# P·V with V as the weights on four column strips, O kept transposed, in a one-core adaLN + sliding-window attention + gMLP kernel

## The chip, the cores and the metric

One NeuronCore of a Trainium2 chip runs the whole program. The metric is the device time of one execution in microseconds, 278.81 us in the median of three runs before the change (278.15 to 280.09). Engine names follow the profile: PE is TensorE's matmul stream, PEld its weight loads, DVE is VectorE, ACT ScalarE, POOL GpSimd, SP SyncE (here only a queue that issues DMAs).

## The reference

One block over x of 2048 tokens by 448: a modulation from c, then attention, then a gMLP.

```python
mod = (_silu(c) @ w_mod)                      # six vectors: sa, ca, ga, sb, cb, gb
h = _layernorm(x) * (1 + ca) + sa
x = x + ga * _A_ref(h, A_wqkv, A_wo)
h = _layernorm(x) * (1 + cb) + sb
x = x + gb * _B_ref(h, B_w_in, B_w_sp, B_b_sp, B_w_out)

# _A_ref: 16 heads of width 28, query i sees keys i-255 .. i
scores = einsum('bhqd,bhkd->bhqk', q, k) * 28 ** -0.5
scores = where((i - j >= 0) & (i - j < 256), scores, -1e9)
o = einsum('bhqk,bhkd->bhqd', softmax(scores), v);  return o @ wo
# _B_ref: z = gelu(x @ w_in); z1, z2 = halves; z2 = layernorm(z2)
#         g = w_sp @ z2 + b_sp;  return (z1 * g) @ w_out
```

## The kernel before

Tokens stand in 16 tiles of 128. The attention works tile by tile (`j`, L794) and in two halves of the heads (L800); a half is two groups of four heads, `qi`. Heads are padded from 28 to 32 columns.

**How the order is set.** The program is a list of steps (`add`, L131), numbered as they are created, each with the engines it may run on and a cost. No loop runs in program order: the string `ORDER` (L19) lists every step as `number.engine.slots`, with p, a, v, g, s for PE, ACT, DVE, POOL and SP, and the slots of the buffers it takes. `order` (L148) replays that list, one in-order program for each engine; `count` and `waits` (L190, L209) derive the semaphores from the steps' dependencies. The costs in the code do not act on the chip; ORDER does.

**Head.** x, the modulation weights and WQ/WK are loaded by SP and ACT (L411 to L421: on ACT's queue first w_mod, then c), DVE and POOL clear pads, and PE runs matmuls on an identity (`warm`, L554). Layernorm statistics (`stats`, L589: `bn_stats`, `bn_aggr`, then two POOL steps at L597 and L600) and `norm` (L606) give xn; PE transposes it (L666), ACT or DVE applies the modulation while copying it to `hT` (L678, L680); then Q, K and V for the 512 tokens (L696, L708, L743, L756), evicted by ACT or DVE (L718/L719, L748/L749, L760/L761). V goes to `Vaug` with a column of ones at place 28 of each head's 32 (L493, L494), so that P·V also gives the softmax's sum.

**Attention of a tile with three key blocks** (j >= 2), for each half:

- S transposed (keys on partitions) for two head groups goes to PSUM banks 0 to 3, one bank for each of the four heads, by 36 matmuls of 32 rows (L858): first 4 of 128 keys by 128 queries for the middle block and 16 of 128 keys by 64 queries, then 16 of 64 keys by 64 queries, which use half of the columns of the array. Only the parts of the two outer blocks that the window can reach are computed. The middle block of the second head group is one more matmul (L867, `QBD` holds Q block-diagonally) into bank 5.
- ACT takes the exponential of both (L819, 2048 and 512 columns) to `PW`. Banks 0 to 3 have one place in rotation (`bW`), so S of the next half waits for this exponential.
- DVE masks the triangles: one pass for each head group, from `PW` to `PT` (`mask_all`, L872, L874).
- PE forms P·V (L901) with P as the weights (128x128) and V as the moving operand (32 columns): three matmuls for each head, 24 in a half, into bank 4 (`bO`, one place).

After both halves DVE takes the reciprocal of the 16 sums (L915), scales O while copying it to `o_sb` (L917), a DMA transpose on SP's queue puts it into `hT` (L923, the issue is at L468), and PE multiplies by wo (L926). x is updated (L931), normalised again, transposed by DMA (L937) and scaled (L949, L951).

**gMLP.** z2 (L1011) and z1 transposed (L1032) with gelu on ACT (L1018, L1040), statistics and normalisation of z2 on DVE (L592, L1023), the spatial product (L1055) and the output product (L1072). z2 shares its place with `PW`, so the gelu waits for all P·V.

Of the kernel before, what the change touches and what calls it, by code (L numbers as in the profile page):

```python
# [19 lines left out]
2.a 24.v 33.g 0.s 25.v 26.v 27.v 36.g 37.g 3.a 1.s 34.g 4.a 31.g 28.v 5.s 35.g 8.a 29.v 38.g 6.s 9.a 7.s 43.a 39.g 53.p.1 54.p.2 55.p.3 44.p.0 130.v  # L20
128.v 131.v 129.v 132.g 45.a 46.a 56.p.4 57.p.5 58.p.6 59.p.7 60.p.2 52.p.1 139.v 137.v 140.v 138.v 133.g 134.v 141.v 136.a.0 142.g 135.a.1 143.v
120.v 145.v.2 108.v 107.v 67.p.3 146.p.2 144.a.3 68.p.0 69.p.4 147.p 150.p.3 40.g 123.g 121.g 122.v 148.v 149.v 151.p 152.a 48.a 70.p.0 71.p.0
154.p.4.5.6.7 155.p 156.p 153.a 158.p 125.g 42.g 160.p 159.p 157.p 162.a 164.a 32.g 41.g 124.g 47.v 10.s 11.s 14.s 127.g 126.v 191.v 192.v 187.v 30.v
49.g 50.g 13.s 15.s 16.s 12.s 161.a 169.p.0 170.a 171.p.1 172.a 346.p.0 347.a.0 163.v 185.v 189.v 186.v 188.v 190.v 51.v 175.p.7 173.p.6 112.p.0
114.p.1 193.g 194.g 199.g 201.g 197.g 200.g.0 195.g 176.v 202.v.1 198.v.2 113.v 196.g.3 350.v 174.a 352.p.0 353.a.1 181.p.7 203.p.0 371.p.0 166.s
167.s 165.s 168.s 17.s 348.v 115.v 206.p.1 177.p.6 204.v 205.v 207.v 109.p.0 372.a.2 373.a 182.a 208.a 378.p.0 379.a.3 380.a 239.v 241.v 243.v 237.v
244.v 110.v 238.v 20.s 19.s 18.s 240.v 242.v 354.v 111.v 178.v 179.p.7 183.p.1 211.p.0 184.v 293.v 356.v 180.v 349.p.0 398.p.0 212.a 351.p 355.p
215.p.1 357.p 400.p.0 209.p.0 399.a.4.0 381.v 291.v 216.v 406.p.0 210.a 245.g 246.g 251.g 252.v.0 358.v 359.v.0 376.v 374.v 253.g 249.g 254.g.1 403.v
221.p.1 213.p.0 383.v 214.v 402.v 294.v 375.p.0 377.p 407.a.5.1 401.a 427.p.0 222.a 408.p.0 382.p 223.p.0 225.p.1 428.a.6.2 435.p.0 409.a 411.v
429.p.0 384.p 258.s 118.g 247.g 250.g.2 256.s 257.s 248.g.3 255.s 262.g 259.g 226.a 436.a.0.3 292.v 224.v 295.v 385.v 386.v.1 229.p.0 227.p.1 404.p.0  # L30
410.v 297.v 228.v 430.a 456.p.0 230.a 457.a.1.4 360.s 218.s 219.s 220.s 217.s 432.v 261.v 260.v 437.p.0 233.p.0 231.p.1 405.p 412.p 296.v 232.v 438.a
234.a 464.p.0 413.p 275.p.1 263.p.0 458.p.0 465.a.2.0 431.v 298.v 116.g 299.g 119.g 300.g 117.g 307.g 305.g 306.g.0 301.g 308.g.1 302.g.2 439.v 414.v
415.v.2 264.v 469.v 440.v 460.v 468.v 276.a 459.a 485.p.0 486.a.3.1 433.p.0 265.p.1 434.p 441.p 466.p.0 493.p.0 266.a 467.a 303.g 304.g.3 442.p
235.p.0 489.v 443.v 444.v.0 494.a.4.2 461.v 487.p.0 269.p.1 514.p.0 236.a 488.a 462.p.0 277.p.0 463.p 470.p 471.p 495.p.0 515.a.5.3 522.p.0 270.v
490.v 497.v 416.s 387.s 472.v 473.v.2 278.a 267.p.1 268.v 498.v 491.p.0 492.p 361.p.0 362.v 523.a.6.4 526.v 363.v 496.a 543.p.0 544.a.0.0 516.p.0
388.p.1 499.p 279.p.0 389.v 548.v 547.v 517.a 280.a 551.p.0 552.a.1.1 500.p 417.p.1 524.p.0 281.p.0 501.v 518.v 418.v 502.v.1 527.v 519.v 525.a 282.a
572.p.0 573.a.2.2 283.p.1 545.p.0 520.p.0 521.p 528.p 529.p 310.s 309.s 445.s 311.s 474.s 312.s 271.s 274.s 273.s 272.s 503.s 580.p.0 284.a 546.a
581.a.3.3 419.v 556.v 555.v 530.v 531.v.0 576.v 364.v 475.p.0 289.p.1 553.p.0 549.p.0 550.p 476.v 601.p.0 554.a 290.a 557.p 574.p.0 558.p 287.p.0
285.p.1 602.a.4.4 477.v 577.v 584.v 420.v 559.v 390.v 560.v.2 478.v 286.v 313.v 391.v 421.v 288.a 575.a 609.p.0 610.a.5.0 504.p.0 314.g 315.g 365.g
366.g 316.g 367.g 368.g.0 578.p.0 323.p.1 582.p.0 479.v 505.v 585.v 605.v 506.v 324.v 630.p.0 583.a 631.a.6.1 446.p.0 579.p 586.p 603.p.0 319.p.1  # L40
587.p 604.a 611.p.0 392.g 480.g 481.g 393.g 394.g 422.g 423.g 395.g.1 396.g 424.v.2 369.v 425.v 447.v 588.v 589.v.1 448.v 614.v 449.v 606.v 613.v
320.a 612.a 638.p.0 639.a.0.2 22.s 532.s 23.s 561.s 21.s 426.s 397.s 317.p.0 329.p.1 632.p.0 607.p.0 659.p.0 318.a 330.v 333.p.0 321.p.1 633.a 642.v
660.a.1.3 322.a 325.s 327.s 328.s 326.s 640.p.0 608.p 641.a 334.v 507.v 634.v 667.p.0 668.a.2.4 664.v 615.p 533.p.0 616.p 562.p.1 661.p.0 643.v 635.v
617.v 618.v.0 563.v 671.v 619.s 688.p.0 662.a 636.p.0 637.p 644.p 645.p 669.p.0 331.p.1 689.a.3.0 696.p.0 670.a 332.a 697.a.4.1 564.v 534.v 646.v
535.v 663.v 647.v.2 693.v 565.v 692.v 536.v 701.v 672.v 335.p.0 337.p.1 690.p.0 665.p.0 338.a 691.a 717.p.0 718.a.5.2 339.p.1 698.p.0 666.p 673.p
674.p 590.s 648.s 828.s 482.g.2 450.g 508.g 451.g 452.g 509.g 537.g 538.g 566.g 539.g 453.g.1 454.g 510.g 340.v 700.v 620.p.1 675.v 483.v 676.v.0
370.s 455.s 540.g.0 567.g 568.g 541.g 814.g 699.a 719.p.0 336.a 720.a 725.p.0 694.p.0 695.p 702.p 703.p 591.p.0 727.p.0 726.a.6.3 728.a 746.p.0
747.a.0.4 721.v 722.v 621.v 704.v 705.v.1 729.v 592.v 730.v 593.v 750.v 622.v 677.s 723.p.0 341.p.1 724.p 731.p 748.p.0 342.a 749.a 754.p.0 732.p
343.p.0 756.p.0 678.p.1 755.a.1.0 757.a 733.v 751.v 623.v 734.v.2 775.p.0 484.s 758.v 759.v 752.p.0 753.p 760.p 761.p 706.s 829.s 542.s 735.s 511.g.1
624.g 569.g.2 512.g 679.v 762.v 763.v.0 777.p.0 776.a.2.1 344.a 778.a 649.p.1 780.v 779.v 650.v 783.p.0 707.p.0 781.p.0 782.p 785.p.0 513.s 812.g  # L50
813.g 811.g 570.g 625.g 626.g 627.g.0 594.v 680.v 681.v 651.v 652.v 784.a.3.2 787.v 786.a 788.v 860.p.0 861.p.1 862.p 789.p 790.p 864.a 653.v 682.g
628.g 683.g 684.g 708.v 685.v.1 595.v 791.v 792.v.1 654.g 655.g 686.g 764.s 571.s 345.s 629.s 736.p.1 765.p.0 656.g.2 817.v 793.s 766.v 767.v 737.v
768.v 818.v 709.v 738.v 815.a 863.p 871.a 878.p.2 879.p.0 880.p 881.p 882.a 889.a 596.g 657.g 597.g 816.g 896.p.3 897.p.1 898.p 899.p 900.a 1012.p.2
794.p.0 914.p.0 907.a 658.s 687.s 769.g 598.g.0 599.g 770.g 600.s 739.v 872.v 710.v 865.v 866.v 711.g 712.g 771.g 713.g 772.v.2 773.v 740.v 741.g
774.s 867.v 795.v 809.g 714.g.1 742.g 796.v 715.v 822.v 884.v 797.v 798.v 891.v 902.v 743.g.0 744.g 799.g 716.s 745.s 800.g 801.v.2 890.v 868.v 883.v
# [210 lines left out]
def bass_adaLN_cond__sliding_block__mixer_gmlp__prompt_kernel(  # L266
# [888 lines left out]
```

## Time and profile before

| | us |
|---|---|
| median of 3 runs | 278.81 (278.15 to 280.09) |
| the profiled execution | 279.08, of which its span is 277.4 |
| PE busy | 266.4 (96%) |
| DVE, ACT, POOL busy | 164.4, 128.2, 127.2 |
| S of the first tile starts; last P·V starts | 18.7; 111.5 |
| first spatial matmul (L1055) | 156.6 |

The granted TensorE clock is 1.00 throughout. The span has three stretches: the head to about 25 us, the attention to about 111 us, in which the products of Q, K and V and the out-projection are mixed in, and then the gMLP. A busy time is the union of the engine's records; small matmuls overlap in the array, so their records' durations add up to more than the time that they take. What a matmul takes is read from the distance of its start to the next one's. In a group's line the numbers after the bar are busy us, mean ns of one, and idle time ahead of it.

### The profile page before, as it was taken

How to read it: one execution, taken by the hardware profiler on the slowest of the kernel's cores; microseconds unless marked ns; L12 is line 12 of the kernel's file. 1: busy time of each engine (PE TensorE's matmuls, PEld its weight loads, DVE VectorE, ACT ScalarE, POOL GpSimd, SP SyncE). 2: the span in 40 equal slices, each digit the busy share in tenths (PEclk: the TensorE clock that was granted, in tenths of full speed). 3: DMA queues.
4: the chain of work that ended last, by engine and by line, in shares of the span. 5: the costliest groups of instructions: out<-in, count | busy, mean ns of one | idle time of the engine just before them, and what ended most of it. 6: DMA issues, size and time to landing. Idle time of an engine off the chain costs nothing.

```text
span 277.4 us, 7383 instructions
## 1 busy us (share of the span) xinstructions
PE 266.4 (96%) x3198; PEld 140.8 (51%) x3225; DVE 164.4 (59%) x364; ACT 128.2 (46%) x154; POOL 127.2 (46%) x191
## 2 busy tenths in 40 slices
PE   4999999999999999999999999999999999999995
PEld 1636466656576766444444444444444444444452
DVE  5679999989989999679798300300320042025434
ACT  2587999999999999577676600000000000000000
POOL 6831826914725669884949000600571065334110
PEclk9999999999999999999999999999999999999999
DMA  7966142145993666834999999100000000001113
GB/s 208 304 170 205 23 91 47 21 80 96 121 225 79 80 80 97 194 77 83 190 176 205 206 197 187 35 0 0 0 2 0 0 0 2 0 0 56 62 50 99
DMA packets 65843, 26.01 MB, mean 94 GB/s; under 512 B 56466, under 2 KB 64723, under 8 KB 65811
## 3 DMA queue, kind: packets, MB, share of 16 engines
q1 hardware_dynamic: 65168, 24.68, 43.4%
q10 hardware_dynamic: 642, 0.86, 1.1%
q8 instruction: 25, 0.41, 0.6%
q14 instruction: 8, 0.06, 0.1%
HBM read 9.01 MB, written 1.84 MB: 39 GB/s over the span
## 4 chain that ended last, share of the span: by engine, by line
PE 82%; DVE 8%; DMA 4%; POOL 3%; issue 1%; ACT 0%; ACTq 0%; SPq 0%; POOLq 0%
PE ps L1055 35%; PE ps L1032 8%; PE ps L1072 7%; PE ps L1011 6%; PE ps L708 5%; PE ps L901 5%; PE ps L858 3%; DMA hT<-xn 3%; PE ps L926 3%; PE ps L756 3%; PE ps L867 2%; DVE st_all L592 2%; PE ps L557 1%; DMA c_row<-in_c_dram 1%; PE ps L696 1%; POOL hT L951 1%
## 5 line engine op out<-in xcount | busy, mean ns | idle before, releaser
L819 ACT ACTIVATE PW<-ps 128x2048 bf16<-128x2048 f32 (+1 forms) x56 | 67.4, 1242 | 2.9 <-PE ps L867 1.1
L1059 DVE TENSOR_TENSOR tmpg<-ps,bsp_bc 128x512 bf16<-128x512 f32 x28 | 19.1, 691 | 83.4 <-PE ps L1055 69.3
L1062 POOL TENSOR_TENSOR z1T<-tmpg,z1T 128x512 bf16<-128x512 bf16 x28 | 31.9, 1153 | 79.3 <-DVE tmpg L1059 79.3
L1055 PE MATMUL ps<-wspB,z 128*128 128x512 bf16 x218 | 49.5, 379 | 0.3
L1055 PE MATMUL ps<-wspA,z 128*128 128x512 bf16 x220 | 48.8, 379 | 0.3 <-issue 0.2
L874 DVE TENSOR_TENSOR PT<-PW,mask 128x1024 bf16<-128x1024 bf16 x56 | 38.9, 721 | 0.7 <-ACT PW L819 0.7
L1055 PEld LDWEIGHTS ps<-wspA,z 128*128 128x128 bf16 x224 | 21.8, 98 | 26.6 <-issue 0.4
L1055 PEld LDWEIGHTS ps<-wspB,z 128*128 128x128 bf16 x224 | 21.9, 98 | 26.2
L600 POOL TENSOR_TENSOR rs_all<-ve_all,neghalf 128x1 f32<-128x1 f32 (+2 forms) x37 | 23.6, 645 | 3.7 <-DVE ve_all L597 3.0
L1011 PE MATMUL ps<-w_in,hT 64*128 64x448 bf16 x224 | 23.0, 349 | 1.2 <-DVE hT L951 0.6
L901 PE MATMUL ps<-Vaug,PT 128*128 128x32 bf16 x496 | 24.1, 177 | 0.1
L901 PEld LDWEIGHTS ps<-Vaug,PT 128*128 128x128 bf16 x496 | 21.8, 96 | 4.0 <-DVE PT L894 0.6
L1032 PE MATMUL ps<-hT,w_in 64*128 64x512 bf16 x196 | 22.5, 376 | 0.0
L1072 PE MATMUL ps<-w_out_g,z1T 128*128 128x448 bf16 x112 | 22.2, 352 | 0.0
L708 PE MATMUL ps<-hT,WQK 128*128 128x512 bf16 x80 | 20.5, 379 | 1.3 <-issue 0.4
L616 POOL TENSOR_SCALAR xn<-x_sb,rs_all,ve_all 128x448 bf16<-128x448 bf16 x21 | 18.1, 863 | 7.0 <-DMA hT<-xn 6.4
L901 PE MATMUL ps<-Vaug,PW 128*128 128x32 bf16 x224 | 20.1, 176 | 0.0
L592 DVE BATCH_NORM_STATS2 st_all<-x_sb 128x6 f32<-128x448 bf16 x32 | 18.9, 610 | 1.6 <-DMA x_sb<-in_A_x_dram 1.5
L592 DVE BATCH_NORM_STATS2 st_all<-z 128x6 f32<-128x448 bf16 x32 | 18.3, 607 | 1.7 <-ACT z L1018 1.7
L901 PEld LDWEIGHTS ps<-Vaug,PW 128*128 128x128 bf16 x224 | 17.6, 96 | 1.9
L597 POOL TENSOR_SCALAR ve_all<-mv_all 128x1 f32<-128x1 f32 (+2 forms) x20 | 6.6, 334 | 25.1 <-DVE mv_all L595 21.5
L1018 ACT ACTIVATE z<-ps 128x896 bf16<-128x896 f32 x16 | 14.1, 916 | 7.8 <-PE ps L1011 6.8
(101 smaller groups left out, 343.9 us busy)
## 6 DMA issues: line engine op xcount, KB each, us to landing
out_dram<-fin SPq DMA_DIRECT2D x16, 112.0 KB, 1.7
x_sb<-in_A_x_dram SPq DMA_DIRECT2D x3, 448.0 KB, 3.9
wmod<-in_w_mod_dram SPq DMA_DIRECT2D x1, 1344.0 KB, 9.5
w_in<-in_B_w_in_dram SPq DMA_DIRECT2D x1, 1344.0 KB, 8.2
QBD<-qT SPq DMA_DIRECT2D x16, 64.0 KB, 2.5
w_out_g<-in_B_w_out_dram SPq DMA_DIRECT2D x1, 784.0 KB, 4.9
bsp_bc<-in_B_b_sp_dram SPq DMA_DIRECT2D x1, 512.0 KB, 5.0
x_sb<-in_A_x_dram SPq DMA_DIRECT2D x2, 224.0 KB, 4.2
```

The lines of the kernel that those rows point to most:

```text
L592: st = [dve(0.62 if True else 0, lambda e, t=t, ci=ci, s=s: e.bn_stats(st_all[:, slot, t, ci, :], s()), deps(t), prio) for ci, s in enumer ...
L600: rs = pool(0.53 + 0.15 * len(tiles), lambda e: e.tensor_tensor(rs_all[:, slot, a:b], ve_all[:, slot, a:b], neghalf[:, 0:b - a], ALU.pow), ...
L708: m = pe(4 * MMS, [lambda e, h=h, g=g, kc=kc, tb=tb: e.matmul(ps[:, h.slot[0], :], lhsT=WQK[:, kc, 4 * g:4 * g + 4, :].rearrange("p a b -> ...
L819: ex = act(xdur, lambda e, out_ap=out_ap, in_ap=in_ap: e.activation(out_ap(), in_ap(), ACT.Exp, scale=SCALE), [s], v - 8.0 + u, takes, tab ...
L874: return dve(0.70, lambda e: e.tensor_tensor(cols(hp.slot[0] * 2048 + 1024 * k, [[256, 4], [128, 2], [1, 128]]), cols(at_w() + 128 + 192 * ...
L901: fns.append(lambda e, hp=hp, hO=hO, hi=hi, bi=bi, kb=kb, hd=hd, nb=nb, a=at[hi][bi], p_of=p_of: e.matmul(ps[:, hO.slot[0], 32 * hd:32 * h ...
L1011: return lambda e, kc, p0, start, stop: e.matmul(ps[:, hs[t % 2].slot[hf], 0:D], lhsT=hT[p0:p0 + 64, kc, t * 128:(t + 1) * 128], rhs=w_in[ ...
L1032: return lambda e, kc, p0, start, stop: e.matmul(ps[:, hs[b // 2].slot[b % 2], :], lhsT=w_in[p0:p0 + 64, kc, ft * 128:(ft + 1) * 128], rhs ...
L1055: m = pe(16 * MMS, [lambda e, h=h, si=si, ft=ft, tb=tb: e.matmul(ps[:, h.slot[0], :], lhsT=z2[:, si, ft * 128:(ft + 1) * 128], rhs=(wspA i ...
L1059: a = dve(0.7, lambda e, h=h, ht=ht, tb=tb: e.tensor_tensor(tmpg[:, ht.slot[0], :], ps[:, h.slot[0], :], bsp_bc[:, tb * 512:(tb + 1) * 512 ...
L1062: u = pool(1.16, lambda e, ht=ht, ft=ft, tb=tb: e.tensor_tensor(z1T[tb][:, ft, :], tmpg[:, ht.slot[0], :], z1T[tb][:, ft, :], ALU.mult), [ ...
L1072: return [lambda e, ft=ft: e.matmul(ps[:, h.slot[0], 0:D], lhsT=z1T[t // 4][:, ft, (t % 4) * 128:(t % 4 + 1) * 128], rhs=w_out_g[:, ft, :] ...
```

## The change

- P·V: V is now the weights (128 keys by 32 columns, one head), P the moving operand, and the four heads of a group stand on the four column strips of the array (`tile_position=(0, 32 * hi)`). A head has five pieces: the middle block (128 queries) and four half blocks (64 queries). For a half that is 40 matmuls, 8 of 128 columns and 32 of 64. The two head groups are one step. The output is O transposed.
- The four half-block pieces read `VX`, copies of V with halves rearranged or blank, made by four DMAs on SP for each 512 tokens (`d_v..`, 16 in all) and cleared by four memsets.
- S: all 56 matmuls of a half are 32 rows by 64 keys, so that one form of the array serves all. The two triangles of each head lie in one 128-column stretch.
- One mask pass in place for a half, with a third mask built by four small copies.
- V's and wo's rows are ordered so that every eighth partition of O transposed is a sum. Ones are written to every eighth column of `Vaug` by one memset (1024 runs of one element on each partition, in place of two with 256 runs each); wo comes by seven DMAs instead of two, into a `wo_g` cleared whole.
- After both halves O is copied from PSUM to `ou` (f32, 128x512; not for the last tile), DVE takes the reciprocal of all 128x512 of it to `rr`, a DMA on SP (`d_r..`) spreads the 16 rows of sums over 128 partitions to `rb`, and DVE or POOL multiplies into `hT`. The DMA transpose of O is gone.
- Head: x's second half is issued first on ACT's queue, c second, w_mod third; w_mod's second part moves to SP.
- `PT` shrinks and shares its place with `w_in`; the loads of `w_in` wait for the first four P·V.

ORDER is new as a whole. Read from it (steps in each, all tiles; "before" is the old string):

| step | before | after |
|---|---|---|
| mask passes on DVE | 64 | 32 |
| reciprocal on DVE | 16 of 128x16 | 16 of 128x512 |
| O scaled | 16 on DVE | 4 DVE, 12 POOL |
| O copied from PSUM | - | 12 DVE, 3 ACT |
| Q, K evictions (L718/719) | 18 ACT, 10 DVE | 9 ACT, 19 DVE |
| K evictions by tile (L748/749) | 2 ACT, 2 DVE | 4 DVE |
| V evictions (L760/761) | 10 ACT, 6 DVE | 2 ACT, 14 DVE |
| first hT (L678/680) | 3 ACT, 5 DVE | 1 ACT, 7 DVE |
| second norm (L616/609), its copy (L619/620) | 12, 11 POOL; 4, 5 DVE | 10, 8 POOL; 6, 8 DVE |
| changes of the array's form in j >= 2 | 84 | 78 |
| identity matmuls between the first transposes of xn | 2 | 0 |

In the new string 10 of the 16 statistics passes over the updated x stand ahead of the last mask on DVE, where the old one has 12.

```diff
-    t_x0 = [load("d_x0%d" % i, "sp", 0.25, ...
+    t_x0 = [load("d_x0%d" % i, ("sp", "act")[i], 0.25, ...
-    t_wo = load2("d_wo", "sp", 0.35, wo_g, ALL, A_wo, ALL, prio=-47.0)
+    t_wo = [load("d_wo%d" % b, "sp", 0.06, lambda e, b=b: e.dma_start(wo_g[b:128:8, :, :], A_wo.rearrange("(g i b) n -> b i g n", g=4, b=7)[b]), (), -47.0) for b in range(7)]
-    t_va = [
-        pool(1.2, lambda e: e.memset(Vaug[:, :, :, DH + 1:32], 0.0), prio=-88.0),
-        pool(1.2, lambda e: e.memset(Vaug[:, :, :, DH:DH + 1], 1.0), prio=-87.0),
-    ]
+    t_va = [pool(1.2, lambda e: e.memset(Vaug[:].rearrange("p t h (a b) -> p (t h a) b", b=8)[:, :, 7:8], 1.0), prio=-88.0)]
...
-                for place in (((0, m, 128, 0, 128, 0, 0),), ((k, o, 128, 0, 64, 128, 0) for k in range(2)), ((k, n, 128, 64, 128, 256, 0) for k in range(2)),
-                              ((k, *e) for k in range(2) for e in ((n, 64, 0, 64, 192, 0), (o + 64, 64, 64, 128, 192, 64)))):
+                for place in (((0, m + p0, 0, 128, 0, p0) for p0 in (0, 64)),
+                              ((k, *e) for k in range(2) for e in ((n, 0, 64, 128, 0), (o, 0, 64, 128, 64), (o + 64, 64, 128, 192, 0), (n + 64, 64, 128, 192, 64),
+                                                                   (n, 64, 128, 256, 0), (o + 64, 0, 64, 256, 64)))):
...
-                mks = [mask_all(k) for k in range(2)]
+                mk = dve(0.72, lambda e, at_w=at_w, cols=cols: e.tensor_tensor(
+                    cols(at_w() + 128, [[512, 4], [192, 2], [1, 128]], PW), cols(at_w() + 128, [[512, 4], [192, 2], [1, 128]], PW),
+                    cols(0, [[0, 4], [0, 2], [1, 128]], mask3), ALU.mult), [exs[0]] + t_mk3, v - 7.0)
...
-                        fns.append(lambda e, ...: e.matmul(
-                            ps[:, hO.slot[0], 32 * hd:32 * hd + 32], lhsT=p_of(a), rhs=Vaug[:, kb, hd, :],
-                            start=(bi == 0), stop=(bi == nb - 1)))
+                        fns.append(lambda e, ...: e.matmul(
+                            ps[32 * hi:32 * hi + 32, hO.slot[0], 128 * qi + q0:128 * qi + q0 + w], lhsT=V[:, 4 * qi + hi, :], rhs=of(hi),
+                            start=first, stop=last, tile_position=(0, 32 * hi)))
...
-        rec = dve(0.25, lambda e, ...: e.reciprocal(rec_all[:, j, :], ov(hO)[:, :, DH]), [lastPV], v - 9.0)
-        t_o = dve(0.63, lambda e, ...: e.tensor_tensor(o_sb ..., ov(hO)[:, :, 0:DH], rec_all ..., ALU.mult), [rec, t_p6], v - 9.0, [ho])
-        oe = turn("d_oT%d" % j, ...
+        if not last:
+            ev = either(0.6, lambda e, bank=bank, raw=raw: e.activation(raw(), bank(), ACT.Copy), 0.69, lambda e, bank=bank, raw=raw: e.tensor_copy(raw(), bank()),
+                        [lastPV, t_wqk], v - 9.0, [hu])
+        of = bank if last else raw
+        rec = dve(0.69 if last else 0.62, lambda e, of=of, inv=inv: e.reciprocal(inv()[:], of()), [lastPV if last else ev, t_wqk], v - 9.0, [hr])
+        rd = add({"sp": (0.6, lambda e, wide=wide, inv=inv, over=over: e.dma_start(wide(), over(inv()[7:128:8, :])))}, [rec], v - 9.0, [hb], dma=name, lat=0.9, tail=2.0)
+        if not last:
+            fo = lambda e, raw=raw, wide=wide, to_h=to_h, q4=q4: e.tensor_tensor(to_h(), q4(raw()), q4(wide()), ALU.mult)
+            oe = add({"dve": (0.62, fo), "pool": (1.2, fo)}, [rd, ev, done], v - 9.0)
```

More of the change, by code (lines that the diff above doesn't have):

```diff
@@ L74 @@
+1115.g 1128.p.3 1134.p.2 1125.p.7 1135.v.1 1129.v.3 1136.s 1130.s 1126.v.0 1127.s 1131.p.6 1132.v.2 1133.s
 """
@@ new lines, in bass_adaLN_cond__sliding_block__mixer_gmlp__prompt_kernel @@
+                cost = 2 * (0.056 + 4 * 0.029) + 0.01
+            fns = []
+            for k, qi in enumerate(qs):
+                pieces = parts(k)
+                for bi, (V, of, q0, w) in enumerate(pieces):
+                    for hi in range(4):
+                        fns.append(lambda e, hO=hO, hi=hi, qi=qi, V=V, of=of, q0=q0, w=w, first=bi == 0, last=bi == len(pieces) - 1: e.matmul(
+                            ps[32 * hi:32 * hi + 32, hO.slot[0], 128 * qi + q0:128 * qi + q0 + w], lhsT=V[:, 4 * qi + hi, :], rhs=of(hi),
+                            start=first, stop=last, tile_position=(0, 32 * hi)))
@@ new lines, in bass_adaLN_cond__sliding_block__mixer_gmlp__prompt_kernel @@
+            halves = [V_half[j // 4], t_vz[(j // 4) % 2]] if nb == 3 else []
+            pv = pe(cost, fns, [mk, exs, lastPV, halves] + [V_ready[kb] for kb in kbs], v + 1, [hO] if half == 0 else [], "cols32")
+            hw.until.append(pv)
+            all_PV.append(pv)
+            lastPV = pv
+        v = 10.0 * j + 7.5
+        done = [[QK_ready[(g, j // 4)] for g in range(4)], [K_ready[(g, 4 * (j // 4) + i)] for g in range(4) for i in ((j % 4,) if j // 4 in FINE else range(4))], [V_ready[j]]]
@@ L925, in bass_adaLN_cond__sliding_block__mixer_gmlp__prompt_kernel @@
+        hb.until.append(oe)
+        chains.append(oe)
         h = Hold(bM)
```

302 lines of the change are left out of this document (160 added, 142 removed).

## The prediction

> **What bounds the kernel now.** I read the busy times by stretch first, then the groups of instructions with their shapes, then the chain of work that ended last.
>
> The stretches (busy us of PE, PEld, DVE, ACT, POOL):
>
> ```profile
> 25.00:111.00 86.00, 84.19 (x2045) 54.75 (x2061) 81.80 (x174) 82.40 (x86) 48.90 (x69) 1.00 0.51 89
> 111.00:118.00 7.00, 6.29 (x74) 2.89 (x68) 4.70 (x13) 3.63 (x6) 5.66 (x14) 1.00 0.85 192
> 118.00:156.60 38.60, 38.20 (x369) 17.98 (x371) 32.34 (x90) 26.49 (x42) 25.01 (x47) 1.00 0.83 152
> ```
>
> See the first line: in the attention PE, ACT and DVE are all at 95 to 98%. Nothing has room but POOL. Relief of one or two of them is worth only what the third allows. After 118 us PE alone is the bound, and the change touches nothing there. So the gain, if any, is made before 118 us and carried unchanged to the end.
>
> The groups that the change touches (busy, mean ns of one):
>
> ```profile
> L819 ACT ACTIVATE PW<-ps 128x2048 bf16<-128x2048 f32 x28 | 52.7, 1883 | 1.6 <-PE ps L858 1.1
> L874 DVE TENSOR_TENSOR PT<-PW,mask 128x1024 bf16<-128x1024 bf16 x56 | 38.9, 721 | 0.7 <-ACT PW L819 0.7
> L901 PE MATMUL ps<-Vaug,PT 128*128 128x32 bf16 x496 | 24.1, 177 | 0.1
> L1059 DVE TENSOR_TENSOR tmpg<-ps,bsp_bc 128x512 bf16<-128x512 f32 x28 | 19.1, 691 | 83.4 <-PE ps L1055 69.3 <-POOL z1T L1062 14.1
> L917 DVE TENSOR_TENSOR o_sb<-ps,rec_all 128x448 bf16<-128x448 f32 x16 | 9.9, 619 | 0.4
> L858 PE MATMUL ps<-qT,KT 32*64 32x64 bf16 x448 | 7.5, 202 | 0.0
> L915 DVE RECIPROCAL rec_all<-ps 128x16 f32<-128x16 f32 x16 | 4.0, 248 | 0.9 <-PE ps L901 0.8
> L548 DVE COPY modT<-ps 128x4 f32<-128x4 f32 x2 | 0.3, 138 | 0.0
> L494 POOL MEMSET Vaug<- 128x256 bf16 x1 | 1.2, 1243 | 0.0
> L521 POOL MEMSET QBD<- 128x1024 f32 x2 | 1.8, 948 | 0.0
> ```
>
> See that mean durations of matmuls (177 to 202 ns) are latencies; their price is the distance of starts. The chain shows it, in the middle of the attention and in the head (start, us, what):
>
> ```profile
> 87.01 0.48 PE ps L858 x36
> 87.49 1.30 PE ps L901 x48
> ```
>
> ```profile
> 9.88 0.43 PE ps L666 x4
> 10.30 0.85 PE ps L557 x2
> 11.16 1.23 PE ps L666 x12
> ```
>
> P.V takes 25 ns a matmul (720 of them, starts 25 ns apart). In an S block single records start 3 to 4 ns apart within a group of strips, and a group of four with 64 columns follows the last after 29 ns. A change of the array's form costs 118 ns inside the block, 123 ns on leaving it, and 83 to 95 ns on entering.
>
> **The change part by part.**
>
> *P.V on PE.* Before, a half takes 24 x 25 ns = 0.60 us. After, it has 10 groups of four strips: two of 128 columns, eight of 64. No row shows 32-column strips. The nearest are the row strips of S: 29 ns for a group with 64 columns, 55 ns with 128, so 2 x 55 + 8 x 29 + 30 to start = 0.37 us, a gain of 0.23 x 28 halves = 6.4 us. The other bound is the 32x64 form of S, where the second group of eight started 53 ns after the first: 2 x 80 + 8 x 53 = 0.58 us, a gain of 0.6. I take the first, which is a steady distance and not that of a first pair.
>
> *S on PE.* Before, 239 ns of starts in a block without the change of form inside it. After, 56 matmuls in seven groups of eight: 66 + 6 x 29 = 240 ns, no gain; bounds 56 x 3.4 = 190 ns (gain 1.4 us in all) and 66 + 6 x 53 = 384 ns (loss 4.1). The forms change 78 times instead of 84, at some 0.11 us: 0.7 gained. PE in all: 7.1 us less, bounds 8.5 less and 2.8 more.
>
> *ACT.* By the new order ACT loses 9 + 2 evictions of Q and K (0.60), 8 of V (0.555), 2 of hT (0.78), and gains 3 copies of O and one hT (0.6, 0.81): 10 us less of 82.4. The exponentials, 28 x (1.883 + 0.60) and 6 x 1.03 = 75.7 us, stay. With them alone a half would last 2.5 us; S blocks now start 2.86 us apart.
>
> *DVE, ahead of the last mask* (busy per instruction, from the groups). Removed: 32 mask passes of 64; 42.7 us become 28 x 0.694 + 4 x 0.74 = 22.4, so -20.3. Fifteen reciprocals and scalings, 15 x (0.25 + 0.62) = -13.1. Two statistics passes and some norms that the order puts later: -2.2. Added: 12 copies of O, 12 x 0.69 = +8.3; two scalings, +1.3; evictions taken from ACT, 9 x 0.68 + 2 x 0.68 + 8 x 0.60 + 2 x 0.52 = +13.3; small clears and copies, +1.6; fifteen reciprocals of 512 columns. No row shows one. The row by size is L1059, 512 f32 columns in 0.68: +10.2. Sum: -0.9 us.
>
> The reciprocal's price is the disputed one. Its only row is 248 ns for 16 columns, where a copy of four from PSUM takes 138; at the 1.09 ns a column between L548's row and L1059's, 16 would take about 150. The 100 ns too much is either paid once or by the column. Once: 0.78 us each, and the sum is +0.6. By the column: (248 - 134) / 16 = 7.1 ns, and 512 columns take 3.8 us. Below, a memset of 1024 f32 takes 0.91, so 512 would be 0.5 and the sum -3.6. Five groups with 448 or 512 f32 columns lie at 0.60 to 0.69 us, so I take 0.68, and keep 3.8 as a rival.
>
> The Trainium skill, VectorE: DVE Perf Modes (Walkthrough, "First, the fixed hardware budget"), says that the reciprocal is an iterative divide "with a repeat count of 8". Read as eight steps of 1.09 ns a column that would be an estimated 4.5 us each instead of 0.68, 3.8 x 15 = 57 us more; the 7.1 ns that the row allows is a little under that, and one size cannot decide it.
>
> So DVE has the same work as before and the other two have 7 and 10 us less. Of 86 us DVE idled 4.2, waiting for ACT's exponentials (L874), for PE (L915, L931) and POOL. With those engines early I let 2.5 of the 4.2 go; bounds 0 and 4.2. What is late next is DVE itself, and so its masks, behind which P.V waits.
>
> *DMA, SP and POOL.* Sixteen transposes of O (issue about 1.3 us each on SP, 3.3 us to landing) go; sixteen spreads, sixteen copies of V and five more loads of wo come, each some 0.6 us of SP: 20.8 us against 22.2, no change, spread over 100 us. The spread waits for DVE's reciprocal; behind it on SP stand the transposes of xn2 for the second norm and Q's DMAs, which have microseconds to spare until 118 us. The scaling waits for the spread (about 2.5 us, the row of the QBD copies), on POOL 12 times; behind it stand norm steps. POOL gains 12 x 1.15 = 13.8 us on 48.9 of 86, so it has room. P.V's bank is free after the copy of O, 0.69, instead of 0.87. P.V of each block of 512 tokens also waits for the four copies of V; they are issued a tile ahead. Cost 0; if the cover goes, one landing of 2.5 us in each of four blocks.
>
> *Head.* The two identity matmuls between the transposes (0.85 us in the chain above) are gone: -0.85. Against it, one memset of 1024 runs of one element replaces two on POOL, ahead of the first statistics. By elements it is the 0.95 of QBD, by runs four times the 1.24 of L494, 5.0. It begins at 2.3 us; the first statistics step now runs at 6.2, and with 5.0 and the mask's memset after it (0.31) it would at 7.6. Between 0 and 1.4 later I take 0.55. Head: -0.3, bounds -0.85 and +0.55. x's second half lands earlier, but DVE works through the first half until 6.1 us anyway; w_mod lands later, but its columns are needed 2 us after they are there.
>
> *Last tile.* The chain from its P.V: before 0.27 + 0.62 + 4.18 (transpose), after 0.78 + 2.5 + 0.69. 1.1 shorter, but PE idles only 0.7 in that stretch: -0.5, bounds 0 and -1.1.
>
> *After it.* DVE has some 3.5 us more there (deferred norms, scalings) in 38.6 us of which 6.3 are idle; the last z2 is done at 154.7, and PE needs it at 156.6. Cost 0, bound 1.6.
>
> Sum: 279.08 (span 277.4 and 1.7 around it) - 0.9 - 2.5 - 0.3 - 0.5 = 274.9. The profiled run is 0.27 above the median of 278.81, so 274.6.
>
> **The rivals.**
>
> *The reciprocal pays by the column.* Then 15 x 3.1 = 47 us more stand on DVE ahead of the last mask, and DVE is the bound: 274.6 + 47 = about 322. It decides as soon as a reciprocal takes more than about 1.0 us (15 x 0.3 eats the 4.2). For it: the 100 ns. Against it: the surplus may be paid once, and every other group of DVE with some 500 f32 columns lies near 0.65. Chance 0.16.
>
> *Nothing is recovered.* DVE stays at 95% because its waits only change names, and the reciprocal takes 0.78: 278.8 + 0.6 - 0.3 - 0.5 = 278.6. For it: DVE's work is the same to 1 us, and three engines hand work round in a ring. Against it: two of the three now have slack. Chance 0.17.
>
> *Groups of strips follow at 53 ns.* PE then has 2.8 us more, at 98% already: about 282. For it: the only pair of 32x64 groups in the trace. Against it: that is a first pair. Chance 0.11, on either side of 1% alike.
>
> *Column strips run one after the other.* By the row of 128 columns (56 ns, L743) and 29 for 64, a half takes 8 x 56 + 32 x 29 = 1.38 us, +0.78 x 28 = 22 us on PE: about 298. Against it: in the 32x64 form two column halves start 3.4 ns apart. Chance 0.04. The Trainium skill, TensorE: Matmul & The Clock Gate ("Wait — 56ns, not 53.3ns?"), has starts never below about 25 ns; by that 40 matmuls would take an estimated 1.0 us and PE would gain 11 us of work. The strips of S, 3 to 4 ns apart, do not obey it.
>
> **How the numbers follow.** The forecast, 274.6, has 0.52; its own range is 269 (all lower bounds: -3.6, -4.2, -0.85, -1.1) to 276. Range for all: 269 to 283, which leaves out the slow reciprocal and the serial strips (0.20). One per cent, about what a measurement of this kernel can tell from no change, is 2.8 us. Faster: 0.52. Within 1%: 0.17 + 0.05 = 0.22. Slower: 0.16 + 0.04 + 0.06 = 0.26.
>
> **What would show it.** The reciprocal's mean: 0.65 to 0.8, or near 4. P.V's 40 matmuls within 0.4 us in the chain. PE's and ACT's busy shares in the attention below 92%, DVE's above 96%. The last P.V starting near 108 instead of 111.5, the first spatial matmul near 152.5. The first statistics step on POOL at 6.2 to 7.6. It would be wrong if DVE's busy time ahead of the last mask differs from before by more than 3 us, or if PE waits for a DMA of V or for the spread.

## The result, and the profile after

The changed kernel takes 323.98 us (median of 4 runs, 322.46 to 325.33), the kernel before 278.81 beside it: a ratio of 1.161, 95% interval 1.154 to 1.168. It is slower by 45 us, where 274.6 was forecast. Times are medians of all runs of a kernel; the intervals leave out one run each of the experiments e3, e6 and e10 that was over 1.5% above the fastest of its kernel, without which these medians would be 313.72, 303.68 and 291.49. The time is within 2 us of the rival "The reciprocal pays by the column", which gave 322 and had a chance of 0.16.

The span grew from 277.4 to 320.7 us. The first spatial matmul starts at 199.5 us instead of 156.6, so 42.9 of the 43.3 lie before it. The busy times by stretch of the changed kernel (busy us of PE, PEld, DVE, ACT, POOL; then the granted clock, the DMA share and GB/s); the first stretch is the one shown of before:

```profile
25.00:111.00 86.00, 69.35 (x2067) 37.60 (x2065) 81.93 (x117) 56.31 (x51) 36.33 (x56) 0.94 0.69 130
111.00:152.00 41.00, 26.59 (x1017) 17.20 (x1016) 38.91 (x46) 21.40 (x18) 19.42 (x29) 0.81 0.65 131
```

DVE alone stays at 95%. PE went from 98 to 81%, ACT from 96 to 65%: DVE holds them up, and does so until 152 us. In the first stretch it gets through 117 instructions where it did 174. The clock granted to TensorE fell to 0.94 and 0.81, where it was 1.00: where PE idles more, it is also clocked lower. What that costs by itself no run separates.

The groups that answer to those of before:

```profile
L851 ACT ACTIVATE PW<-ps 128x2048 bf16<-128x2048 f32 x28 | 52.6, 1877 | 31.5 <-PE ps L896 31.2
L955 DVE RECIPROCAL rr<-ou 128x512 f32<-128x512 f32 x15 | 50.1, 3339 | 0.1
L910 DVE TENSOR_TENSOR PW<-PW,mask 128x1024 bf16<-128x1024 bf16 x28 | 20.0, 730 | 0.0
L951 DVE COPY ou<-ps 128x512 f32<-128x512 f32 x12 | 8.1, 677 | 0.4 <-PE ps L930 0.4
L896 PE MATMUL ps<-qT,KT 32*64 32x64 bf16 x1344 | 17.9, 203 | 10.8 <-issue 10.8
L930 PE MATMUL ps<-PW,Vaug 128*32 128x128 bf16 x224 | 12.6, 241 | 5.1 <-DVE PW L910 3.0 <-DMA VX<-Vaug 1.9 <-DVE ou L951 0.2
L496 POOL MEMSET Vaug<- 128x1024 bf16 x1 | 4.7, 4662 | 0.0
```

The reciprocal takes 3.34 us, not 0.68. The one mask (0.73) and the copy of O (0.68) cost what was forecast. And there is something that the sum had no term for: the S matmuls wait 10.8 us for "issue", that is for nothing that the profile shows. Before, PE had next to none of it. The chain has both, in the middle of the attention (start, us, what):

```profile
103.40 3.26 DVE rr L955
106.66 0.56 DVE KT L763
107.21 0.05 issue
107.26 0.93 PE ps L970 x4
108.19 0.60 PE ps L896 x56
108.78 0.46 PE ps L930 x40
109.24 0.32 PE ps L905
109.56 1.51 PE ps L770 x8
111.08 0.27 PE ps L896 x27
111.34 0.71 issue
```

A block of P.V, 40 matmuls, takes 0.46 us in all: the strips run side by side. But a block of S stops in its middle, after 27 of 56 matmuls.

### The profile page after: what moved, and what is told of

It is laid out like the page before. It is cut to its first block, busy times and chain, and to the rows that moved or that the text cites. A ratio compares the mean times of both kernels' runs of the same rounds, so it can differ in the third digit from the quotient of the medians.

```text
span 320.7 us, 9487 instructions
## 1 busy us (share of the span) xinstructions
PE 279.9 (87%) x4232; PEld 140.7 (44%) x4232; DVE 209.5 (65%) x362; ACT 126.8 (40%) x142; POOL 131.4 (41%) x194
## 4 chain that ended last, share of the span: by engine, by line
PE 67%; DVE 20%; issue 5%; POOL 2%; DMA 2%; ACT 2%; SPq 1%; DVEq 0%; POOLq 0%
PE ps L1101 30%; DVE rr L955 10%; PE ps L1118 7%; PE ps L1078 7%; PE ps L1057 6%; PE ps L722 4%; PE ps L770 3%; PE ps L896 2%; DMA VX<-Vaug 2%; DVE PW L910 2%; PE ps L930 2%; PE ps L970 2%; POOL Vaug L496 1%; ACT PW L851 1%; DVE ou L951 1%
## 5 line engine op out<-in xcount | busy, mean ns | idle before, releaser
L851 ACT ACTIVATE PW<-ps 128x2048 bf16<-128x2048 f32 (+1 forms) x56 | 69.0, 1237 | 46.6 <-PE ps L896 31.2
L955 DVE RECIPROCAL rr<-ou 128x512 f32<-128x512 f32 x15 | 50.1, 3339 | 0.1
L896 PE MATMUL ps<-qT,KT 32*64 32x64 bf16 (+1 forms) x1568 | 20.4, 209 | 13.7 <-issue 12.8
L722 PE MATMUL ps<-hT,WQK 128*128 128x512 bf16 x96 | 26.0, 406 | 5.5 <-DVE x_sb L975 3.8
L961 POOL TENSOR_TENSOR hT<-ou,rb 128x512 bf16<-128x512 f32 x12 | 16.2, 1347 | 33.8 <-DMA rb<-rr 33.8
L613 POOL TENSOR_TENSOR rs_all<-ve_all,neghalf 128x1 f32<-128x1 f32 (+2 forms) x37 | 23.5, 649 | 10.7 <-DVE ve_all L610 10.0
L896 PEld LDWEIGHTS ps<-qT,KT 32*64 32x64 bf16 x1568 | 15.5, 106 | 24.9 <-issue 18.0
L1128 DVE TENSOR_TENSOR fin<-ps,x_sb 128x448 bf16<-128x448 f32 x16 | 9.7, 621 | 24.9 <-PE ps L1118 24.9
L610 POOL TENSOR_SCALAR ve_all<-mv_all 128x1 f32<-128x1 f32 (+2 forms) x20 | 5.6, 283 | 42.4 <-DVE mv_all L608 42.2
L970 PE MATMUL ps<-wo_g,hT 128*128 128x448 bf16 x64 | 16.8, 389 | 4.9 <-DVE KT L763 2.3
L910 DVE TENSOR_TENSOR PW<-PW,mask 128x1024 bf16<-128x1024 bf16 x28 | 20.0, 730 | 0.0
L1064 ACT ACTIVATE z<-ps 128x896 bf16<-128x896 f32 x16 | 13.9, 915 | 10.7 <-PE ps L1057 10.6
```

What stands on the lines that cost most here:

```text
L613: rs = pool(0.53 + 0.15 * len(tiles), lambda e: e.tensor_tensor(rs_all[:, slot, a:b], ve_all[:, slot, a:b], neghalf[:, 0:b - a], ALU.pow), ...
L722: m = pe(4 * MMS, [lambda e, h=h, g=g, kc=kc, tb=tb: e.matmul(ps[:, h.slot[0], :], lhsT=WQK[:, kc, 4 * g:4 * g + 4, :].rearrange("p a b -> ...
L851: ex = act(xdur, lambda e, out_ap=out_ap, in_ap=in_ap: e.activation(out_ap(), in_ap(), ACT.Exp, scale=SCALE), [s], v - 8.0 + u, takes, tab ...
L896: fm.append(lambda e, hm=hm, k=k, qi=qi, key=key, lo=lo, hi=hi, col=col, p0=p0, t=t, j=j: e.matmul(ps[p0:p0 + 64, hm.slot[t], k * 192 + co ...
L910: mk = dve(0.72, lambda e, at_w=at_w, cols=cols: e.tensor_tensor(cols(at_w() + 128, [[512, 4], [192, 2], [1, 128]], PW), cols(at_w() + 128 ...
L955: rec = dve(0.69 if last else 0.62, lambda e, of=of, inv=inv: e.reciprocal(inv()[:], of()), [lastPV if last else ev, t_wqk], v - 9.0, [hr])
```

## The experiments

My first theory was that the reciprocal explains all of the loss. Its rival was that the strips, the copies of V or the blocks of S carry part of it.

**1. A product in place of the reciprocal** (e1).

```
-  e.reciprocal(inv()[:], of())
+  e.tensor_tensor(inv()[:], of(), of(), ALU.mult)
```

> The changed kernel with the 512-column reciprocal replaced by a product of the sums with themselves, of the same 128x512 f32 shape (a plain copy for the last tile, from PSUM); everything else, the order of the work included, is left. It leaves out the inverse, so O is not divided by its sums. Theory: the reciprocal's 3.34 us in place of the predicted 0.68 is the whole of the loss. The product should take 0.65 to 0.8 us; 15 x 2.6 = 39 us and some 2.6 us of the last tile come off, 324 - 42 = 282, and with PE's clock back near 1.00 down to the 274.6 of the prediction: 272 to 284. Rival: the column strips, the copies of V or the longer groups of S carry a good part of the loss; then DVE's work goes but another wait takes its place and the time stays over 295.

The product in the reciprocal's place:

```profile
L955 DVE TENSOR_TENSOR rr<-ou 128x512 f32<-128x512 f32 x15 | 11.8, 788 | 0.1
```

Measured: 311.41 us, ratio 1.111 (1.104 to 1.118), on the rival's side. The product took 0.79 us, DVE's busy time fell from 209.5 to 172.9, and only 12.6 of 45 us came back. The theory fell: something else keeps the kernel at 311 once DVE is free.

**2. The reciprocal added to the kernel before** (e2).

```
+  e.reciprocal(ones_f[:], ones_f[:])      # 128x512, sixteen times
```

> The kernel before, with nothing of the change, plus one reciprocal of a 128x512 f32 tile of ones, in place, ahead of each of the sixteen small reciprocals; its result is used nowhere. Theory: the reciprocal pays by the column whatever is in the tile, 3.3 us each (16 x 3.3 = 53 us), DVE was busy 114 of the 125 us between 25 and 150, so some 42 to 53 us show: 318 to 332, about as slow as the changed kernel. Rival: the kernel before hides most of it because PE, ACT and POOL have work of their own there: under 300.

The added reciprocals:

```profile
L916 DVE RECIPROCAL ones_f<-ones_f 128x512 f32<-128x512 f32 x16 | 53.6, 3347 | 5.2 <-PE ps L902 5.2
```

Measured: 333.28 us, ratio 1.191 (1.185 to 1.197), just over the range: 53.2 us more, with 53.6 us of reciprocals. On an engine at 95% all of it shows. So the reciprocal by itself is able to make the whole loss, and yet taking it away returned a quarter.

**3. Half the columns** (e3).

```
-  e.reciprocal(inv()[:], of())
+  e.reciprocal(inv()[:, 0:256], of()[:, 0:256]); e.tensor_copy(inv()[:, 256:512], of()[:, 256:512])
```

> The changed kernel with the reciprocal taken of the first 256 columns alone; the other 256 are copied, so that half of O is not divided by its sums. Theory (a price by the column, through 248 ns for 16 and 3339 ns for 512): 248 + 240 x 6.23 = 1743 ns for 256; with a copy of some 0.3 us 15 x 1.3 = 20 us come off: 300 to 307. Rival: a price paid in another way, such as a fixed price for any tile of this size, leaves the 256 columns at over 2.5 us and the time above 312.

The reciprocals of this run and of the next (128x64):

```profile
L955 DVE RECIPROCAL rr<-ou 128x256 f32<-128x256 f32 x15 | 26.1, 1743 | 0.1
```

```profile
L960 DVE RECIPROCAL rr<-ou 128x64 f32<-128x64 f32 x16 | 8.7, 541 | 0.1
```

Measured: 315.18 us, ratio 1.124 (1.115 to 1.132). The duration is the forecast 1743 ns to the nanosecond; with 541 for 64 columns and 3339 for 512 the price is 6.2 to 6.3 ns a column and some 0.15 us. The time is 8 us over the range, and above the 312 of the rival, whose fixed price the duration rules out: it approaches the same floor near 311.

**4. The change with a cheap inverse** (e4). O leaves PSUM transposed in blocks of 32x32, so that a tile has 64 columns of sums. ORDER is rewritten with it, and e6 to e8 keep that order.

```
-  e.tensor_copy(raw(), bank());  e.reciprocal(inv()[:], raw());  spread by DMA;  product
+  e.transpose(raw(), bank());  e.reciprocal(low(), raw()[:, 7::8]);  product by low() broadcast;  e.transpose(hT, product)
```

> A version of the change that keeps P.V on column strips but inverts each sum once: DVE transposes O in blocks of 32x32 on its way out of PSUM, so that the sums of a tile stand in 64 columns in place of 512; the reciprocal takes these 64; POOL multiplies with the inverse broadcast along 8 columns, and a second transpose by DVE writes hT. The copy out of PSUM and the spread by DMA go. It computes all of the reference. Theory: the 64 columns take 148 + 64 x 6.23 = 547 ns, the transposes about 0.7 and 0.4 us; against the product version DVE has some 0.5 us a tile more, 8 us, of which part shows: 272 to 286, and if the chain of the last tile without a DMA saves its 3.5 us, at the lower end. Rival: the transposes by DVE cost over 1.5 us each, or POOL's strided product over 2.5 us, and the time is above 295.

Measured: 311.89 us, ratio 1.116 (1.110 to 1.121), where 272 to 286 was expected. It is on the rival's side of 295, but not for the rival's reason: the transposes take 0.71 and 0.69 us (the second was given 0.4) and POOL's product 1.18. The reciprocal is cheap, and the time is that of e1. So the 311 is no matter of the missing inverse in e1.

I then looked at where PE pauses. The trace also has the transfers of the queue of kind "instruction", 16 KB each; the page of the changed kernel counts 33:

```profile
q8 instruction: 33, 0.54, 0.8%
```

They fit TensorE's program in blocks of 256: 8464 records are 33.1 such blocks, and the kernel before has 25 transfers for 6423 records, 25.1 blocks. In e1, 16 pauses of PE over 0.45 us (from one start to the next), 23.2 us in all, end 1.2 to 1.9 us after such a transfer has landed, and the last seven distances between them are 256 records of TensorE each, to one. The transfers follow each other by 3.3 us at the least (3.26 in e3, 3.45 in e1), and in the attention of the kernel before their median distance is 5.1 us. The new theory: the change has more instructions (PE and PEld 8464 records instead of 6423) and each is shorter, so that TensorE comes to the end of a block of 256 before the next is there. The rival: only the matmuls' own time counts.

**5. More instructions in the kernel before** (e5).

```
+  tiny = [... e.matmul(ps[0:128, hm.slot[t], 0:2], ...) for _ in range(9) for t in range(4)]
+  fm = tiny + fm
```

> The kernel before with 36 small matmuls more ahead of each block of S (2 columns each, 9 on each strip of 32 rows, their results overwritten by the block itself), 28 blocks: 28 x 36 x 2 = 2016 instructions of TensorE more with their weight loads, about as many as the change adds (the trace has PE 3198 to 4208 and PEld 3225 to 4232). Theory: TensorE's program comes in blocks of 16 KB, 256 instructions, and in the version with the product each block took at least 4.1 us from the crossing of the one ahead until it could be used; 2016 / 256 = 7.9 blocks x 4.1 = 32 us more where the kernel before had blocks at 5.1 us, of which it hides some: 296 to 315, with idle times of PE whose releaser is issue inside the blocks of S. Rival: only the time of the matmuls counts, 36 x 8.4 ns = 0.30 us, 28 x 0.30 = 8.5 us: 286 to 290.

Measured: 295.67 us, ratio 1.059 (1.054 to 1.063): 16.1 us more, between the two. The trace has ten pauses of the kind described, 10.6 us together, where the kernel before has one of 0.7; with the 8.5 us of the matmuls' own time they overshoot 16.1 by 3. The supply costs, but about half of what I gave; the rest does not show in the time.

**6 and 7. Fewer instructions** (e6: S in 40 matmuls; e7: P.V in 24 as well).

```
-  ... (n, 0, 64, 128, 0), (n, 64, 128, 256, 0), (o + 64, 64, 128, 192, 0), (o + 64, 0, 64, 256, 64) ...
+  ... (n, 0, 128, 128, 0, step 128), (o + 64, 0, 128, 256, 64, step -64) ...
   e7:
-  (vx(1), at(side + 128, 64), 0, 64), (vx(2), at(side + 128, 64), 64, 64)
```

> The version with the transpose first, with S in 40 matmuls a half instead of 56: the two pieces of one key block that go to two places of PSUM are one matmul whose output steps over (the four triangles stay side by side, mask and two of the copies of V are turned accordingly). It computes all of the reference. 28 x 16 x 2 = 896 instructions of TensorE fewer. Theory (supply of instructions): 3.5 blocks of 256 fewer at 4.1 to 5 us: 14 to 17 us off 312, 294 to 299. Rival: the matmuls' own time alone, 16 x 8.4 ns x 28 = 3.8 us: 306 to 310.

> The same, and P.V without its two last pieces (the full 64x64 blocks of the neighbouring tile: those keys are left out of the output), 24 matmuls a half instead of 40: another 896 instructions fewer. Theory: another 3.5 blocks, 14 to 17 us, until another engine is the bound: 279 to 288. Rival: 16 x 8.8 ns x 28 = 3.9 us more than the merged version: not under 300 if that one is at 306 to 310.

Measured: 304.61 us (ratio 1.085, 1.078 to 1.092) and 296.98 (1.060, 1.057 to 1.064), both between theory and rival. Some 7.5 us for 896 instructions each, twice the matmuls' own time and half of the theory's.

**8. Without the copies of V** (e8, on the version of e6).

```
-  e.dma_start(both(vx(0, 0), 8 * row, n), both(vo(0, a, b), 0, n))      # and three like it
+  e.dma_start(vx(0, 0)[0:1, 0:64], vo(0, a, b)[0:1, 0:64])
```

> The merged version with the copies of V cut to 128 bytes each; P.V takes its weights from V itself in the same shape, so that three of its five pieces have wrong keys. All instructions stay. Theory: the copies (16 issues, 5.5 us each to landing, 128 to 512 KB) cost in two ways, by the wait of PE for the first of a block of tiles (4 to 8 us in the traces) and by making the loads of instructions late; 6 to 12 us off the merged version: 284 to 292. Rival: the copies are hidden or only their one wait counts: within 4 us of the merged version.

Measured: 297.17 us, ratio 1.062 (1.058 to 1.066), some 7 us less: within the 6 to 12 expected to come off, though not within the range of times, which stood on a lower time for e6. The copies cost, too.

**9. POOL's order** (e9, on the version of e6: the product moved back to its old place).

> The merged version with one thing moved: POOL's product with the inverse stands in POOL's order where the changed kernel has its product, and no longer right behind the reciprocal. It computes all of the reference. In the merged version POOL stood up to 14.7 us in front of this product while the statistics of the next tiles were queued behind it, and PE waited 9.2 us for what hangs on them, with the clock at half for some 10 us. Theory: that part of its time is this order's own: 8 to 14 us off 304.6, 291 to 297. Rival: another wait takes its place: over 301.

Measured: 300.70 us, ratio 1.076 (1.069 to 1.084), 3 to 4 us less where 8 to 14 were expected. More was moved than the one thing: in the new ORDER three of the products go to DVE, and DVE's second transposes stand elsewhere. It is the fastest version with all of the reference's work and the change's idea, and still 21 us behind the kernel before.

**10. Strips alone** (e11: S and masks as before, P.V on strips, the inverse as in e4).

> P.V on column strips alone: S in 36 matmuls and with two masks into a buffer of its own, as in the kernel before; P.V with V as weights in three pieces of 128 columns a head (24 matmuls a half, no copies of V); O out of PSUM by DVE's transpose, the reciprocal of 64 columns, product on POOL, second transpose. It computes all of the reference. TensorE has about as many instructions as before. Theory: no idle time by issue, no copies to wait for; DVE has 56 masks of 0.7 us again and some 0.8 us a tile more than the kernel before (two transposes of 0.69 and 0.4 and the reciprocal's 0.55 for 0.25 and 0.63), 12 us on an engine that was at 91%: 279 to 292. Rival: the strips themselves cost the time: over 296.

Measured: 309.46 us, ratio 1.108 (1.105 to 1.112), a miss. It has neither more instructions nor copies, but DVE is busy 196.8 us where the kernel before has 164.4. Its two lines that I had priced too low or left out:

```profile
L920 DVE TENSOR_TENSOR VX<-PW,mask 128x1024 bf16<-128x1024 bf16 x56 | 41.3, 783 | 0.0
L970 DVE STREAM_TRANSPOSE hT<-rb 128x512 bf16<-128x512 bf16 x16 | 10.9, 687 | 0.1
```

DVE is busy 82.5 of the 86 us from 25 to 111 and all of the 19 us after that, so its 32.4 us more account for the 30 us of the run. I had left out the evictions that the new order takes from ACT (13.3 in the prediction's own sum). The run does not show what the strips cost by themselves; e12 below, which has them too, takes no longer than the kernel before.

**11 to 16. All eight combinations.** Three suspects: the reciprocal (or a product), the instructions (S 56 and P.V 40, or 40 and 24) and the copies of V (or 128 bytes each). The changed kernel and e1 are two of the eight.

> The version with the product in place of the reciprocal (the order of the work as in the changed kernel), with S in 40 matmuls and P.V in 24: 1792 instructions of TensorE fewer. It leaves out the inverse and the keys of two of five pieces of P.V. Theory: what is left of the loss after the reciprocal is mostly TensorE's supply of instructions; its idle times of that kind summed to 22.7 us in 15 places between 39 and 148 us, and go: 311.4 - 15 (the two steps as measured on the other version) to 311.4 - 26: 285 to 296. Rival: these steps overlap with the clock and with waits for DVE, and less than 10 us come off: over 301.

> As the version with the product, S in 40 and P.V in 24 matmuls, and the copies of V cut to 128 bytes each (P.V takes its weights from V itself: wrong keys). It leaves out the inverse, keys and copies. Theory: the three causes (reciprocal, supply of instructions, copies) are all: about 7 us under the run with the copies, 276 to 289, near the kernel before and the 274.6 of the prediction. Rival: something else of the change costs 10 us or more: over 290.

> The changed kernel with its 512-column reciprocal, but with S in 40 and P.V in 24 matmuls a half and the copies of V cut to 128 bytes: the reciprocal alone of the three causes. It leaves out keys and copies. Theory, the causes overlap: without any of them (279.5) DVE was busy 94 of 97 us between 33 and 130, so 15 x 2.58 (3.34 less 0.76) + 2.6 = 41 us more of DVE show nearly whole: 314 to 321. Rival, the causes add: the reciprocal cost 324.0 - 311.4 = 12.6 with the other two there, so 279.5 + 12.6 = 292: 288 to 297.

> The version with the product, S in 56 and P.V in 40 matmuls, the copies of V cut to 128 bytes: the 1792 instructions of TensorE more alone. It leaves out the inverse and the copies. Theory: they cost less when no copies are beside the loads of TensorE's program: 291 to 299 (10 to 19 over 279.5, in idle times of PE by issue at every 256th instruction). Rival: the supply of instructions matters only together with the copies: under 286.

> The changed kernel with reciprocal and copies, S in 40 and P.V in 24 matmuls. It leaves out keys. Theory (overlap): DVE sets the time, 315 to 322, little under the changed kernel's 324. Rival (the causes add): 292.0 + 12.6 = 305: 301 to 309.

> The changed kernel with reciprocal and all its matmuls, the copies of V cut to 128 bytes. It leaves out the copies. Theory (overlap): 316 to 323. Rival (the causes add): 324.0 - 12.4 = 312: 308 to 314.

Medians in us, and the ratio to the kernel before with its interval:

| | with the reciprocal | with a product |
|---|---|---|
| many instructions, copies | 323.98 (1.154 to 1.168) | 311.41 (1.104 to 1.118) |
| many instructions, no copies | 322.25 (1.149 to 1.158) | 300.69 (1.069 to 1.082) |
| few instructions, copies | 323.15 (1.149 to 1.162) | 291.97 (1.038 to 1.049) |
| few instructions, no copies | 322.93 (1.150 to 1.162) | 279.53 (1.000 to 1.005) |

All six rivals are out. e10, e12 and e16 came within their ranges, e13, e14 and e15 one to two us above theirs.

The columns differ in kind. On the right the two other costs add: the instructions 21.2 and 19.4 us, the copies 10.7 and 12.4. On the left they vanish: 322 to 324 whatever else is there. The reciprocal alone costs 43.4 us, its 41 us of DVE time (15 x 2.58 and 2.7 for the last tile) and a little more, and hides the rest. That is why taking it away first returned only 12.6. The last cell takes as long as the kernel before, to 0.2%, although it leaves out work of the reference.

What stands behind each cell. The reciprocal alone (e13), PE's waits between 25 and 165 us; they name DVE, masks first:

```profile
PE ps L931 <- DVE PW L912: 12.4, 3, 4.6
PE ps L722 <- DVE x_sb L976: 4.6, 2, 3.0
```

The copies (e10), the same view: three blocks of tiles waited for theirs:

```profile
PE ps L931 <- DMA VX<-Vaug: 10.7, 3, 5.4
PE ps L898 <- issue: 2.0, 2, 1.2
```

The instructions (e14), the chain:

```profile
100.13 0.24 PE ps L896
100.37 2.00 issue
102.36 0.64 PE ps L896 x47
```

This pause lies at record 4800 of TensorE; the transfer of its block began at 99.68, landed at 100.85, and PE went on 1.5 us later. There are 13 pauses of this kind, and 11 of them lie a multiple of 256 records apart, to one. They sum to 18.0 us, of 21.2. The matmuls' own time would be some 7.7 us more by the prices of e6 and e7, and the granted clock stands at a half for 13.6 us between 25 and 150, where e12 has 3.4. These add to more than 21.2, so they overlap, and how the 21.2 divide among them is not shown. The Trainium skill, Runtime: NRT & Kernel Launch (Instruction fetch mechanics), says that engines fetch their program in blocks of 16 KB, 256 instructions, while they run the one before, and that the cost of crossing is "mostly hidden". The blocks are in these traces; hidden it was in the kernel before (one pause of 0.7 us), not here.

None of them (e12), the stretch from 25 to 111 us:

```profile
25.00:111.00 86.00, 78.55 (x2151) 44.59 (x2161) 83.09 (x160) 75.98 (x67) 63.04 (x80) 0.98 0.62 126
```

DVE is at 97%, PE at 91, ACT at 88. From these shares, what the change took from PE and ACT could not be used.

## Why the prediction was wrong, point by point

- **The reciprocal, 0.68 us: the step that failed.** It was priced by the row nearest in size (L1059, a product), with the operation's own row beside it. That row, 248 ns for 16 columns, allowed 7.1 ns a column; measured are 6.2, 3.34 us, so 15 x 2.66 = 40 us more on DVE than the sum had, and all of it shows (e13). The rival had the mechanism and the place. It got 0.16 because "every other group of DVE with some 500 f32 columns lies near 0.65", which speaks of other operations. That its sum (322) is so close is in part luck: its price of 3.8 was 7 us too much over the 15, its base of 274.6 was 5 us under the 279.53 of e12, and the 2.7 us of the last tile were not in it. The page of the Trainium skill that the prediction named, VectorE: DVE Perf Modes (Walkthrough, "First, the fixed hardware budget"), read as eight steps, gave an estimated 4.5 us; the trace agrees with its direction, three quarters of its size.
- **P.V on PE, 0.37 us a half: right.** 336 ns from the first to the last start, with groups of four strips 28 or 29 ns apart after 64 columns and 56 to 66 after 128, as read from the rows of S. In the chain, which counts the last matmul to its end, a block takes 0.46 us and not "within 0.4". The rival of serial strips (298) is out. The Trainium skill, TensorE: Matmul & The Clock Gate ("Wait — 56ns, not 53.3ns?"), has starts never below about 25 ns; on column strips they are 336 / 39 = 8.6 ns apart on average here, and the measurement decides.
- **S on PE, 240 ns a block, at most 384: wrong, 457 where nothing interrupts it.** The starts inside a group of strips are 3.4 ns apart, as read, but only for the first 32 matmuls with their loads; then comes a step of 101 ns, and the other 24 follow at 8.4 ns. And no term said what 112 instructions cost that pass in half a microsecond. The 1792 instructions more cost 21.2 us in e14, with pauses for the supply of the program that sum to 18.0. With the reciprocal it does not show.
- **Copies of V, "Cost 0; if the cover goes, one landing of 2.5 us in each of four blocks": the cover goes.** The 10 us of that bound are what e10 and e12 give, 12.4; the landing takes 5.5 us in the changed kernel (6.4 in e10), and three blocks waited.
- **DVE ahead of the last mask, -0.9; recovered, -2.5.** With all three causes out the kernel takes 279.53, and DVE is busy 97% of the attention (95 before). That is the rival "Nothing is recovered" (278.6), not the forecast, and it is the second step that failed. That slightly dearer masks (0.80 in e12, 0.694 in the sum) eat the rest is argued, not shown.
- **Head, -0.3: 0.** The first Q/K matmul starts at 12.64 instead of 12.87 us, but S of the first tile at 18.65 instead of 18.69. POOL's memset goes by runs, 4.66 us, near the upper bound of 5.0, and the first statistics step came at 7.12.
- **Last tile, -0.5:** from the last P.V to the first spatial matmul 47.5 us instead of 44.5, with PE busy 45.3 of them; small beside the rest, and not taken apart.
- **SP and POOL, 0: right.** POOL waits 33.8 us for spreads, and PE for none of them; in e12 PE waits once, 1.7 us, for POOL's product.

## What to carry to other kernels

Price an operation by its own row first, even if that row is thirty times smaller: two sizes of the same operation, or one and the assumption that it pays by the column, bound it better than another operation of the right size. One small row is a rough bound: the same 128x16 reciprocal took 194 ns in e2, and by the prediction's working that would have been 3.8 ns a column instead of 7.1. On an engine at 95% multiply what is added by the count and take it as lost time (e2 and e13 here). When an edit replaces long instructions by many short ones, ask how long 256 of TensorE's last: here the transfers of such blocks came no closer than 3.3 us, and the kernel with a median of 5.1 us had next to no pauses. And when one cause is found, take the others out as well before calling it the cause, because the slowest engine hides what the others lose.

## What the runs showed of the hardware that was not expected

- The reciprocal on DVE: 541 ns for 64 columns, 1743 for 256, 3339 for 512, whether from SBUF or PSUM (3358).
- TensorE's program comes 16 KB at a time, no closer than 3.3 us, and after a pause of this kind PE resumes 1.2 to 1.9 us after a block has landed. The pauses were 0.5 to 4.3 us.
- The granted clock goes with idle time of PE: 1.00 before, 0.93 in e2, which adds work to DVE alone, 0.95 over the changed kernel, 0.81 between 111 and 152 us. In the records it drops to a half for 3.4 us or a multiple of it, in the changed kernel six times between 40 and 150 us, though no two matmul starts in the 7 us ahead lie more than 2.9 us apart.
- DVE transposes 128x512 in blocks of 32x32 in 0.70 us from f32 in PSUM and in 0.69 from bf16 in SBUF (e11): half the bytes do not halve it.
